# Gate logits with rows of x as the weights, a later place for four low parts, and one earlier quarter of W2: a fused attention and experts kernel

## The chip, the cores and the metric

One core of one Trainium2 chip runs the whole program. The metric is the device time of one execution in microseconds (us); the median of three runs is given. Five engines work from queues of their own: TensorE (PE, with its weight loads shown apart as PEld), VectorE (DVE), ScalarE (ACT), GpSimd (POOL) and SyncE (SP), which issues the DMAs here.

## The reference, cut to what matters

```python
# attention: batch 4, heads 8, sequence 576, head size 64, 128 features
def phi(x):
    proj = np.einsum('bhsd,df->bhsf', x, w_phi)
    proj = proj - np.max(np.abs(proj), axis=-1, keepdims=True)
    return np.concatenate([np.exp(proj), np.exp(-proj)], axis=-1)
q_p, k_p = phi(q), phi(k)
kv, z = np.einsum('bhsf,bhsd->bhfd', k_p, v), np.sum(k_p, axis=2)
num = np.einsum('bhsf,bhfd->bhsd', q_p, kv)
den = np.einsum('bhsf,bhf->bhs', q_p, z)[..., None] + 1e-06
x = num / den                      # as 2304 tokens x 512
# gated MLP
x = ((x @ w1) * (x @ w2) @ w3) @ w_out      # w1, w2 512x1024, w3 1024x1024, w_out 1024x512
# experts: 8 of them, every token goes through all
P = np.exp(x @ w_gate - (x @ w_gate).max())  # w_gate 512x8; then 8 rounds of row and column scaling
out = sum(P[:, e:e+1] * (np.maximum(x @ w1[e], 0) @ w2[e]) for e in range(8))  # w1[e] 512x1024, w2[e] 1024x512
```

## The kernel before, in words

Every float32 matrix is split into a high part in the reduced format fp32r and a low part (the difference), and a product is three fp32r matmuls: high x high, low x high, high x low (`mm3`, lines 84 to 87). ACT mostly makes the high part (`copy`), DVE the low one (`subtract`).

**Attention** (to about 214.6 us) goes through steps of three sequence tiles, k and q in turn. PE projects (`pp`), DVE takes the largest absolute value and the difference (`m`, `d`, in `st_M`), ACT makes the exponentials (`e`), PE sums `kv`. For q, PE transposes `d` (`dt`), ACT makes `q`, PE makes the denominators `dn` and the numerators `nu`. ACT copies each finished `kv` out of PSUM as `kh` and `kz`. PSUM banks of one pool of four turn among `kv`, `dt`, `dn` and `nu`. Beside it, the program already prepares the weights of the MLP: `get_w12(n)` for n below NW = 4 unpacks a weight into a ring of buffers (`wring`), makes its high part `wH` on ACT and its low part `wL` on DVE.

**Gated MLP** (214.6 to 531 us): six blocks j of 384 tokens. In each, 8 units `ab_unit(j, ft)` multiply x (its high and low parts XH and XL) with w1 and w2, then `px` matmuls give the new x, which ACT and DVE split again into XH and XL. `logits` follows: for each of four pieces of x's 512 rows the 16 columns of the split gate (`WG`) are the weights and 384 tokens of x move through (`lg`); DVE copies the 16x384 result (`lgs`), and PE transposes it in three pieces into one PSUM tile `lp`, tokens by gates. Blocks 0, 1 and 2 do so after their px matmuls, blocks 3 to 5 together after the last block.

**Experts**: units u, each one quarter of an expert's hidden layer, in chunks of 768 tokens. Units 0 to 15 are experts 0 to 3 of chunk 0 (531 to 785 us). From unit 16 (`NUC`) on, W2 is also taken in quarters: a quarter K11, K21 or K22 is loaded raw (`load_k`), split into a tile `t` (`load_t`) and stored for the later chunks. One raw buffer (`kr`) serves all of them. `products(u)` does seven products of Strassen's kind (a11, s2, s3, s1, a22, a12, s4); its weights `w_u_0` and `w_u_1` come by DMA, `w_u_2` is converted in the kernel (`get_w1(u, 2)`), behind an earlier copy by `issue_after(first[0])`. `part` then makes the split hidden operands `ah`, `al`, `bh`, `bl`, `dh`, `dl`, `eh`, `el` of the unit. After every fourth unit (p = 3) PE multiplies those of all four with the tiles t, group by group: first K11 with ah and al, then K21 with bh and bl. The raw `w_19_2` lies in a quarter of the tile MT, as it did before.

The order within each engine's queue is that of the program text, moved by priorities of a scheduler; `tc.issue_after(x)` keeps an instruction behind x.

Of the kernel before, what the change touches and what calls it, by code (L numbers as in the profile page):

```python
# [8 lines left out]
F32 = mybir.dt.float32  # L9
# [13 lines left out]
def f32(ap):  # L23
    return ap.bitcast(F32)
# [3 lines left out]
def kernel(  # L28
# [49 lines left out]
    def x_at(p, kt, c0, n):  # L78
        i, o = divmod(c0, NH)
        return XHL[i][p][:, kt, o : o + n]  # L80
# [15 lines left out]
    def subtract(key, out, a, b, i=0):  # L96
        engine(key, i).tensor_tensor(out, a, b, ALU.subtract)
# [565 lines left out]
    with ExitStack() as c2:  # L663
# [19 lines left out]
        def w12_piece(n):  # L683
            ft, w = divmod(n, 2)
            if n < NW:
                t = W12E[n]
            else:
                r = rb.tile([P, DF], U32, name=f"rw{n}", tag="r")
                nc.sync.dma_start(r, w12i[ft][:, w * DM : (w + 1) * DM].bitcast(U32))
                r = r.rearrange("p (n x) -> p n x", x=2)  # L690
                t = ring()
                u = t.bitcast(U32)
                with tc.issue_after(last["k"]):
                    nc.scalar.activation(t, r[:, :, 1].bitcast(F32), AF.Copy, scale=2.0**-112)
                nc.vector.tensor_scalar(
                    u, u, 3, 0x7FFFFFFF, ALU.logical_shift_left, ALU.bitwise_and
                )
                nc.vector.scalar_tensor_tensor(
                    u, r[:, :, 0], 29, u, ALU.logical_shift_right, ALU.bitwise_or
                )  # L700
                nc.vector.scalar_tensor_tensor(
                    u, r[:, :, 1], 0x80000000, u, ALU.bitwise_and, ALU.bitwise_or
                )
            pool = w12a if n < 9 else w12p
            hi = pool.tile([P, KT, P], F32R, name=f"wH{n}")
            lo = pool.tile([P, KT, P], F32R, name=f"wL{n}")
            t = t.rearrange("p (k f) -> p k f", k=KT)
            copy("wh", hi, t, n)
            subtract("wl", lo, t, f32(hi), n)
            w12[n] = hi, lo  # L710

        def get_w34(i):
# [15 lines left out]
            nc.vector.tensor_tensor(WG[:, :, 1], wg, f32(WG[:, :, 0]), ALU.subtract)  # L728

        def logits(blocks):  # L730
            got = []
            for j in blocks:
                ps = px_p.tile([P, N1], F32, name=f"lg{j}", tag="px")[0 : 2 * NE]
                for kt in range(KT):
                    w = WG[:, kt].rearrange("p a e -> p (a e)")
                    nc.tensor.matmul(ps, w, x_at(0, kt, j * N1, N1), start=kt == 0, stop=False)
                    nc.tensor.matmul(ps, w, x_at(1, kt, j * N1, N1), start=False, stop=kt == KT - 1)
                lg = xt_p[-1].tile([P, N1], F32, name=f"lgs{j}", tag="xt" if len(xt_p) == 1 else "lg")[0 : 2 * NE]
                nc.vector.tensor_copy(lg, ps)
                got.append((j, lg))  # L740
            for j, lg in got:
                for i in range(N1 // P):
                    nc.tensor.transpose(
                        lp[:, j * N1 // P + i].rearrange("p a e -> p (a e)"),
                        lg[:, i * P : (i + 1) * P],
                        ident[0 : 2 * NE, 0 : 2 * NE],
                    )

        cH = [cp.tile([P, N1], F32R, name=f"cH{i}") for i in range(FT)]
        cL = [cp.tile([P, N1], F32R, name=f"cL{i}") for i in range(FT)]  # L750
# [29 lines left out]
        for j in range(NT // N1):  # L780
            c0 = j * N1
            CH = [*zip(cH, cL)]
            if j == 1:
                CH[0] = cE
            for ft in range(FT):
                if j == 1 and ft == 0:
                    continue
                behind = ab_unit(j, ft, *CH[ft])
                if j == 0 and ft == FT // 2:
                    ab_unit(1, 0, *cE)  # L790
                if j > 0 and (ft < FT - 1 if 1 < j < NT // N1 - 1 else j == 1 or ft % 2 == 0):
                    sum_next(behind)
            if c0 + N1 == NT:
                assert made[0] == len(jobs)
                c7.close()
                c3.close()
                xt_p.append(sbuf(c2, "xt6", KT))
                xc = sbuf(c4, "xc", side="left")
                wc1 = sbuf(c4, "wc1", 2, "left")
                rwb = sbuf(c4, "rwb", side="left")  # L800
                c6 = c4.enter_context(ExitStack())
                rw1 = sbuf(c6, "rw1", 2, "left")
                load_w1(0)
                load_w1(1)
                prep_x(0, sbuf(c2, "xs0").tile([P, 2, N1], F32, name="xs0"))
                for u in range(2):
                    for i in range(3):
                        get_w1(u, i)
            if j == 0:
                get_gate()  # L810
            for dt in range(KT):
                ps = px_p.tile([P, N1], F32, name=f"px{j}_{dt}", tag="px")
                dc = slice(dt * P, (dt + 1) * P)
                for ft in range(FT):
                    hi, lo = w34[ft]
                    mm3(ps, hi[:, dc], lo[:, dc], *CH[ft], ft == 0, ft == FT - 1)
                xt = xt_p[-1].tile([P, N1], F32, name=f"xt{j}_{dt}", tag="xt")
                nc.scalar.copy(xt, ps)
                i, o = divmod(c0, 2 * N1)
                nc.sync.dma_start(XS[i][:, dt, o : o + N1], xt)  # L820
                xh, xl = x_at(0, dt, c0, N1), x_at(1, dt, c0, N1)
                nc.scalar.copy(xh, xt)
                with tc.high_priority(60) if c0 + N1 == NT else nullcontext():
                    behind = nc.vector.tensor_tensor(xl, xt, f32(xh), ALU.subtract).ins
                if 0 < j < NT // N1 - 1:
                    sum_next(behind)
            if c0 < NH:
                logits([j])
            elif c0 + N1 == NT:
                logits(range(NH // N1, NT // N1))  # L830
            if j == 0:
                c5.close()
                tq.append(sbuf(c7, "tq", 2))
                for k in range(3):
                    sum_load(k)
            if c0 + N1 == NH:
                cx[0].close()
                ones = sbuf(c4, "on", side="left").tile([P, P], F32, name="ones")
                nc.vector.memset(ones, 1.0)
                rx = sbuf(c4, "rx", side="left")  # L840
                load_x(0)
                tq.append(sbuf(c7, "tq1", 2, "left"))
                turn[0] = made[0]
                for k in range(3):
                    sum_load(made[0] + 3 + k)
# [5 lines left out]
    with c4:  # L851
# [49 lines left out]
        def products(u, bank, between):  # L901
# [17 lines left out]

            product("a11", B11, (c11, None))  # L920
            if NUC < u + 1 < NU and (u + 1) % NP > 1:
                with tc.issue_after(first[0]):
                    get_w1(u + 1, 2)
            product("s2", T2, (c12, c11))
            product("s3", T3, (c21, c12))
# [126 lines left out]

        rawK = {}

        def load_k(e, k):
            if e == NE:
                return
            r = rawK[e, k] = kr.tile([P, NP, DH], F32, name=f"k{e}_{k}", tag="k")
            j, h = KB[k]
            w = moe2_w2[e].rearrange("(j n p) (h d) -> j h p n d", j=2, p=P, h=2)[j, h]  # L1060
            nc.sync.dma_start(r, w)
# [7 lines left out]
        def load_t(u, k, taken=False):  # L1069
            s, e, p = units[u]  # L1070
            if not taken:
                take_t(u, k)
            t = TK[k]
            if s > 0 or k not in KB:
                nc.sync.dma_start(f32(t), W2S[e][:, WK[k]])
                return
            r = rawK.pop((e, k))
            copy("W2h", t[:, :, 0], r)
            subtract("W2l", t[:, :, 1], r, f32(t[:, :, 0]))
            load_k(e + (k == K22), {K11: K21, K21: K22, K22: K11}[k])  # L1080
            nc.sync.dma_start(W2S[e][:, WK[k]], f32(t))

        LATE = []
# [41 lines left out]
        def operands(u):  # L1125
            for i, c in enumerate(products(u, lambda n: bank(n)[:, 0:N1], lambda behind: None)):
                part(u, i, c)
# [9 lines left out]
        for u, (s, e, p) in enumerate(units):  # L1137
            if u < NUC:
                continue
            if p == 0:  # L1140
                take_mt(u)
                load_w1(u + NP - 1)
            operands(u)
            store_ready()
            if p < NP - 1:
                if u == NUC:
                    for k in (K11, K21, KT4):
                        take_t(u, k)
                    load_t(u, KT4, True)
                elif u < NUC + NP:  # L1150
                    load_t(u, (None, K11, K21)[p], True)
                elif p < 2:
                    load_t(u, p + 1)
                continue
# [155 lines left out]
```

## Time and profile before

| what | value |
|---|---|
| median of 3 runs | 1982.31 us (1982.3 to 1982.49) |
| profiled execution | 1983.45 us |
| its span, first to last instruction | 1981.7 us |
| PE busy | 1962.0 us (99%), 14037 matmuls |
| PE weight loads busy | 1874.9 us (95%) |
| DVE busy | 1471.1 us (74%) |
| ACT busy | 828.4 us (42%) |
| granted TensorE clock | 1.000 |

The span is what the trace covers; the profiled execution is 1.75 us longer. Busy is the union of an engine's instructions; the weight loads run beside the matmuls and are counted apart. The shares are means over stages that differ.

### The profile page before, as it was taken

Reading aid. Unit: us, or ns where it says so; the run is one execution under the profiler, and the core shown is the slowest. Engines: PE = TensorE matmul, PEld = TensorE weight load, DVE = VectorE, ACT = ScalarE, POOL = GpSimd, SP = SyncE. Lnnn points to the kernel's source line nnn. Section 1 sums busy time; section 2 is a strip of 40 time slices with the busy share of each in tenths; the row PEclk is TensorE's granted clock in tenths of the full one; section 3 lists DMA queues with packets and bytes.
Section 4 is the critical chain, followed back from the end, with each engine's and each line's share of the span. In section 5 each row is a group of like instructions: output and inputs, shape, how many; then the busy total and the mean of one; then the engine's idle time right before and its main releaser. Section 6 shows DMA issues by size and latency. Waiting matters only on the chain.

```text
span 1981.7 us, 35200 instructions
## 1 busy us (share of the span) xinstructions
PE 1962.0 (99%) x14037; PEld 1874.9 (95%) x14037; DVE 1471.1 (74%) x2546; ACT 828.4 (42%) x1539; POOL 93.2 (5%) x122
## 2 busy tenths in 40 slices
PE   8999999999999999999999999999999999999999
PEld 6677899999988988999999999999999999999999
DVE  7977946676798666888786777666788666777666
ACT  6866723344434432444343433333444333433333
POOL 2543100000000000000000000000000000000000
PEclk9999999999999999999999999999999999999999
DMA  6452538899899889888887777777778777777774
GB/s 224 161 168 94 170 138 288 309 312 330 305 349 333 291 320 315 306 290 307 314 307 269 245 250 246 251 245 254 246 276 283 244 245 253 245 250 252 244 247 150
DMA packets 187011, 511.55 MB, mean 258 GB/s; under 512 B 13792, under 2 KB 68960, under 8 KB 168800
## 3 DMA queue, kind: packets, MB, share of 16 engines
q1 hardware_dynamic: 186480, 508.88, 74.6%
q8 instruction: 111, 1.82, 0.4%
q10 hardware_dynamic: 368, 0.43, 0.1%
q14 instruction: 52, 0.43, 0.1%
HBM read 371.88 MB, written 137.36 MB: 257 GB/s over the span
## 4 chain that ended last, share of the span: by engine, by line
PE 89%; DVE 5%; DMA 3%; ACT 1%; issue 1%; SPq 0%; POOL 0%; DVEq 0%; ACTq 0%
PE ps L85 6%; PE ps L87 6%; PE ps L86 6%; PE pa L85 5%; PE pa L86 5%; PE pa L87 5%; PE b L1181 4%; PE b L1183 4%; PE b L1182 4%; PE ab L87 3%; PE ab L85 3%; PE ab L86 3%; PE a L1181 3%; PE a L1183 3%; PE a L1182 3%; PE py L86 2%
## 5 line engine op out<-in xcount | busy, mean ns | idle before, releaser
L917 DVE TENSOR_TENSOR c<-c,ps 128x384 f32<-128x384 f32 x480 | 255.8, 549 | 56.4 <-PE ps L87 53.8
L1202 DVE SCALAR_TENSOR_TENSOR o<-mt,Pw,o 128x512 f32<-128x512 f32 x108 | 75.1, 747 | 142.2 <-ACT mt L1192 142.2
L915 ACT COPY c<-pa 128x384 f32<-128x384 f32 x96 | 45.6, 475 | 228.2 <-PE pa L87 175.8
L1181 PE MATMUL b<-t,dh 128*128 128x256 f32 x480 | 136.0, 283 | 0.0
L1182 PE MATMUL b<-t,dh 128*128 128x256 f32 x480 | 135.8, 283 | 0.0
L1183 PE MATMUL b<-t,dl 128*128 128x256 f32 x480 | 135.8, 283 | 0.0
L87 PE MATMUL ab<-XH,wL 128*128 128x384 f32 x384 | 130.1, 339 | 0.0
L85 PE MATMUL ab<-XH,wH 128*128 128x384 f32 x384 | 130.0, 338 | 0.0
L86 PE MATMUL ab<-XL,wH 128*128 128x384 f32 x384 | 130.0, 338 | 0.0
L1108 ACT ACTIVATE c<-c 128x384 f32<-128x384 f32 x80 | 42.0, 525 | 169.8 <-DVE c L917 169.8
L917 DVE TENSOR_TENSOR c<-c,pa 128x384 f32<-128x384 f32 x192 | 103.6, 550 | 10.6 <-PE pa L87 9.6
L1181 PEld LDWEIGHTS b<-t,dh 128*128 128x128 f32 x480 | 92.1, 192 | 0.3 <-ACT mt L1192 0.3
L1183 PEld LDWEIGHTS b<-t,dl 128*128 128x128 f32 x480 | 92.2, 192 | 0.0
L1182 PEld LDWEIGHTS b<-t,dh 128*128 128x128 f32 x480 | 92.1, 192 | 0.0
L1181 PE MATMUL a<-t,eh 128*128 128x256 f32 x320 | 90.7, 283 | 0.7 <-DMA t<-w2s 0.7
L1183 PE MATMUL a<-t,el 128*128 128x256 f32 x320 | 90.6, 283 | 0.0
L1182 PE MATMUL a<-t,eh 128*128 128x256 f32 x320 | 90.5, 283 | 0.0
L1095 DVE SCALAR_TENSOR_TENSOR bl<-c,bh 128x768 fp32r<-128x768 f32 x80 | 76.3, 953 | 10.1 <-ACT bh L1094 10.1
L86 PE MATMUL py<-w,hH 128*128 128x512 f32 x192 | 76.3, 398 | 0.0
L87 PE MATMUL py<-w,hL 128*128 128x512 f32 x192 | 76.1, 397 | 0.0
L85 PE MATMUL py<-w,hH 128*128 128x512 f32 x192 | 75.5, 397 | 0.0
L1094 ACT ACTIVATE bh<-c 128x768 fp32r<-128x768 f32 x80 | 67.7, 846 | 14.3 <-DVE c L917 13.7
(287 smaller groups left out, 6513.5 us busy)
## 6 DMA issues: line engine op xcount, KB each, us to landing
t<-w2s SPq DMA_DIRECT2D x128, 1024.0 KB, 4.8
w<-w1s SPq DMA_DIRECT2D x160, 512.0 KB, 5.0
w<-w1s SPq DMA_DIRECT2D x64, 768.0 KB, 6.1
tr<-in_moe_w_dram SPq DMA_DIRECT2D x48, 512.0 KB, 5.2
w1s<-w SPq DMA_DIRECT2D x32, 768.0 KB, 7.4
w1s<-w SPq DMA_DIRECT2D x32, 512.0 KB, 7.9
w2s<-w SPq DMA_DIRECT2D x48, 256.0 KB, 7.8
w2s<-t SPq DMA_DIRECT2D x12, 1024.0 KB, 7.5
```

The source lines that it names most:

```text
L85: nc.tensor.matmul(ps, aH, bH, start=start, stop=False)
L86: nc.tensor.matmul(ps, aH, bL, start=False, stop=False)
L87: return nc.tensor.matmul(ps, aL, bH, start=False, stop=stop).ins
L915: first[0] = nc.scalar.copy(o, ps).ins
L917: nc.vector.tensor_tensor(o, t, ps, ALU.add)
L1094: nc.scalar.activation(hi, src, AF.Relu)
L1095: nc.vector.scalar_tensor_tensor(lo, src, 0.0, f32(hi), ALU.max, ALU.subtract)
L1108: nc.scalar.activation(c22, c22, AF.Relu)
L1181: nc.tensor.matmul(dst[i], H[:, c], T[:, 0], start=f, stop=False, skip_group_check=True)
L1182: nc.tensor.matmul(dst[i], H[:, c], T[:, 1], start=False, stop=False, skip_group_check=True)
L1183: nc.tensor.matmul(dst[i], L[:, c], T[:, 0], start=False, stop=l, skip_group_check=True)
L1202: nc.vector.scalar_tensor_tensor(o, src[i], w, o, ALU.mult, ALU.add)
```

## The change

Three edits. `logits` no longer takes the gate as the weights: each tile of 128 tokens of x (high, then low part, four pieces) is loaded as weights and the 16 gate columns move through, so that tokens by gates come out directly in `lp`; the transposes and the copies `lgs` are gone. Logits of blocks 0 and 1 are issued after the second unit of the next block. The low parts of the first four weights of `get_w12` are issued after the last `d` of attention. In chunk 0, for expert 4, the raw quarter K21 is loaded into free columns of MT ahead of the unit and K22 into the raw buffer; K11 and K21 are converted around unit 16 rather than in units 16 to 18, and `w_19_2` no longer waits for the copy.

```diff
--- before.py
+++ after.py
@@ -706,7 +706,8 @@
             lo = pool.tile([P, KT, P], F32R, name=f"wL{n}")
             t = t.rearrange("p (k f) -> p k f", k=KT)
             copy("wh", hi, t, n)
-            subtract("wl", lo, t, f32(hi), n)
+            with tc.issue_after(last["d"]) if n < NW else nullcontext():
+                subtract("wl", lo, t, f32(hi), n)
             w12[n] = hi, lo
 
         def get_w34(i):
@@ -728,23 +729,12 @@
             nc.vector.tensor_tensor(WG[:, :, 1], wg, f32(WG[:, :, 0]), ALU.subtract)
 
         def logits(blocks):
-            got = []
-            for j in blocks:
-                ps = px_p.tile([P, N1], F32, name=f"lg{j}", tag="px")[0 : 2 * NE]
+            for t in (j * N1 // P + i for j in blocks for i in range(N1 // P)):
+                o = lp[:, t].rearrange("p a e -> p (a e)")
                 for kt in range(KT):
                     w = WG[:, kt].rearrange("p a e -> p (a e)")
-                    nc.tensor.matmul(ps, w, x_at(0, kt, j * N1, N1), start=kt == 0, stop=False)
-                    nc.tensor.matmul(ps, w, x_at(1, kt, j * N1, N1), start=False, stop=kt == KT - 1)
-                lg = xt_p[-1].tile([P, N1], F32, name=f"lgs{j}", tag="xt" if len(xt_p) == 1 else "lg")[0 : 2 * NE]
-                nc.vector.tensor_copy(lg, ps)
-                got.append((j, lg))
-            for j, lg in got:
-                for i in range(N1 // P):
-                    nc.tensor.transpose(
-                        lp[:, j * N1 // P + i].rearrange("p a e -> p (a e)"),
-                        lg[:, i * P : (i + 1) * P],
-                        ident[0 : 2 * NE, 0 : 2 * NE],
-                    )
+                    nc.tensor.matmul(o, x_at(0, kt, t * P, P), w, start=kt == 0, stop=False)
+                    nc.tensor.matmul(o, x_at(1, kt, t * P, P), w, start=False, stop=kt == KT - 1)
 
         cH = [cp.tile([P, N1], F32R, name=f"cH{i}") for i in range(FT)]
         cL = [cp.tile([P, N1], F32R, name=f"cL{i}") for i in range(FT)]
@@ -788,6 +778,8 @@
                 behind = ab_unit(j, ft, *CH[ft])
                 if j == 0 and ft == FT // 2:
                     ab_unit(1, 0, *cE)
+                if c0 < NH and ft == min(j, 1) and j > 0:
+                    logits([j - 1])
                 if j > 0 and (ft < FT - 1 if 1 < j < NT // N1 - 1 else j == 1 or ft % 2 == 0):
                     sum_next(behind)
             if c0 + N1 == NT:
@@ -824,7 +816,7 @@
                     behind = nc.vector.tensor_tensor(xl, xt, f32(xh), ALU.subtract).ins
                 if 0 < j < NT // N1 - 1:
                     sum_next(behind)
-            if c0 < NH:
+            if c0 + N1 == NH:
                 logits([j])
             elif c0 + N1 == NT:
                 logits(range(NH // N1, NT // N1))
@@ -919,7 +911,7 @@
 
             product("a11", B11, (c11, None))
             if NUC < u + 1 < NU and (u + 1) % NP > 1:
-                with tc.issue_after(first[0]):
+                with tc.issue_after(first[0]) if u + 1 != NUC + NP - 1 else nullcontext():
                     get_w1(u + 1, 2)
             product("s2", T2, (c12, c11))
             product("s3", T3, (c21, c12))
@@ -1052,10 +1044,12 @@
 
         rawK = {}
 
-        def load_k(e, k):
+        def load_k(e, k, r=None):
             if e == NE:
                 return
-            r = rawK[e, k] = kr.tile([P, NP, DH], F32, name=f"k{e}_{k}", tag="k")
+            if r is None:
+                r = kr.tile([P, NP, DH], F32, name=f"k{e}_{k}", tag="k")
+            rawK[e, k] = r
             j, h = KB[k]
             w = moe2_w2[e].rearrange("(j n p) (h d) -> j h p n d", j=2, p=P, h=2)[j, h]
             nc.sync.dma_start(r, w)
@@ -1077,7 +1071,10 @@
             r = rawK.pop((e, k))
             copy("W2h", t[:, :, 0], r)
             subtract("W2l", t[:, :, 1], r, f32(t[:, :, 0]))
-            load_k(e + (k == K22), {K11: K21, K21: K22, K22: K11}[k])
+            if e > EARLY[0]:
+                load_k(e + (k == K22), {K11: K21, K21: K22, K22: K11}[k])
+            elif k != K21:
+                load_k(e + (k == K22), {K11: K22, K22: K11}[k])
             nc.sync.dma_start(W2S[e][:, WK[k]], f32(t))
 
         LATE = []
@@ -1139,16 +1136,22 @@
                 continue
             if p == 0:
                 take_mt(u)
+                if u == NUC:
+                    r = MT[0][:, 0:2].rearrange("p a n -> p (a n)")[:, 0 : NP * DH]
+                    load_k(e, K21, r.rearrange("p (a n) -> p a n", a=NP))
                 load_w1(u + NP - 1)
+                if u == NUC:
+                    for k in (K11, K21, KT4):
+                        take_t(u, k)
+                    load_t(u, KT4, True)
+                    load_t(u, K11, True)
             operands(u)
             store_ready()
             if p < NP - 1:
                 if u == NUC:
-                    for k in (K11, K21, KT4):
-                        take_t(u, k)
-                    load_t(u, KT4, True)
+                    load_t(u, K21, True)
                 elif u < NUC + NP:
-                    load_t(u, (None, K11, K21)[p], True)
+                    pass
                 elif p < 2:
                     load_t(u, p + 1)
                 continue
```

What stands on PE at the end of block 5, before the first product of unit 0 (pa, a11): the last logits matmuls and the transposes before, then the same place of the change.

```order
2160 L736 MATMUL lg_6047<-XH_68,WG 16x384
2161 L737 MATMUL lg_6047<-XL_69,WG 16x384
2162 L736 MATMUL lg_6047<-XH_68,WG 16x384
2163 L737 MATMUL lg_6047<-XL_69,WG 16x384
2164 L743 MATMUL lp<-ident,lgs_6034 128x16 x3
2165 L743 MATMUL lp<-ident,lgs_6045 128x16 x3
2166 L743 MATMUL lp<-ident,lgs_6056 128x16 x3
2167 L85 MATMUL pa_6130<-a11h_5843,w_0_2_5883 128x384
```

```order
2235 L736 MATMUL lp<-WG,XH_68 128x16
2236 L737 MATMUL lp<-WG,XL_69 128x16
2237 L736 MATMUL lp<-WG,XH_68 128x16
2238 L85 MATMUL pa_6190<-a11h_5873,w_0_2_5913 128x384
2239 L86 MATMUL pa_6190<-a11l_5874,w_0_2_5913 128x384
2240 L737 MATMUL lp<-WG,XL_69 128x16
2241 L736 MATMUL lp<-WG,XH_68 128x16
2242 L87 MATMUL pa_6190<-a11h_5873,w_0_2_5913 128x384
2243 L85 MATMUL pa_6190<-a11h_5873,w_0_2_5913 128x384
2244 L737 MATMUL lp<-WG,XL_69 128x16
```

The 24 matmuls of 384 columns and nine transposes became 72 of 16 columns. The later ones stand among the first matmuls of unit 0; this piece shows where they begin to.

What stands on ACT at the end of attention, behind the last cast of the four weights `wH` (e_2801 is the exponential of the last k piece, kh_2859 and kz_2860 are the copies of head pair 15's kv, L694 unpacks further weights into the ring), before and then in the change.

```order
221 L94 COPY kh_2804<-kv_2738 128x256
222 L94 COPY kz_2805<-kv_2738 128x128
223 L226 ACTIVATE q_2647<-dt_0_2775 128x2x192 x2
224 L226 ACTIVATE q_2781<-dt_1_2782 128x2x192 x2
225 L94 CAST XH_68<-x_2588 128x576
226 L205 ACTIVATE e_2801<-d_2731 128x768 x2
227 L694 ACTIVATE wring<-rw_3022 128x512
228 L694 ACTIVATE wring<-rw_3045 128x512
229 L694 ACTIVATE wring<-rw_3073 128x512
230 L94 COPY kh_2859<-kv_2808 128x256
231 L94 COPY kz_2860<-kv_2808 128x128
232 L226 ACTIVATE q_2781<-dt_0_2845 128x2x192 x2
```

```order
221 L205 ACTIVATE e_2801<-d_2731 128x768 x2
222 L226 ACTIVATE q_2647<-dt_0_2775 128x2x192 x2
223 L226 ACTIVATE q_2781<-dt_1_2782 128x2x192 x2
224 L94 CAST XH_68<-x_2588 128x576
225 L94 COPY kh_2804<-kv_2738 128x256
226 L94 COPY kz_2805<-kv_2738 128x128
227 L694 ACTIVATE wring<-rw_3022 128x512
228 L226 ACTIVATE q_2781<-dt_0_2845 128x2x192 x2
229 L694 ACTIVATE wring<-rw_3045 128x512
230 L226 ACTIVATE q_2781<-dt_1_2851 128x2x192 x2
231 L94 CAST XH_68<-x_2689 128x576
232 L94 COPY kh_2859<-kv_2808 128x256
```

The exponential moved to the front, and the copies kh and kz of both head pairs moved behind activations for q; those of pair 15 now stand behind the cast XH_68 of x_2689 too.

What stands on SP in chunk 0 when the loads of unit 18's weights (w_18_0, w_18_1) come (k_0, k_1 and k_5 are the raw quarters K11, K21 and K22 of expert 4, mt_8376 and mt_8436 the tile MT), before and then in the change.

```order
393 L1061 DMA k_0_8374<-in_moe_w_dram 128x4x256
394 L559 DMA mt_8376<-in_moe_w_dram 128x768
395 L1075 DMA t_4_2_8464<-w2s_167 128x2048
396 L574 DMA w_18_0_8412<-w1s_4_119 128x2x512
397 L574 DMA w_18_1_8422<-w1s_4_119 128x2x512
398 L1061 DMA k_1_8558<-in_moe_w_dram 128x4x256
399 L1081 DMA w2s_167<-t_4_0_8462 128x2048
```

```order
393 L1055 DMA k_0_8434<-in_moe_w_dram 128x4x256
394 L1055 DMA mt_8436<-in_moe_w_dram 128x4x256
395 L559 DMA mt_8436<-in_moe_w_dram 128x768
396 L1069 DMA t_4_2_8441<-w2s_167 128x2048
397 L1055 DMA k_5_8445<-in_moe_w_dram 128x4x256
398 L1078 DMA w2s_167<-t_4_0_8439 128x2048
399 L574 DMA w_18_0_8482<-w1s_4_119 128x2x512
400 L574 DMA w_18_1_8492<-w1s_4_119 128x2x512
```

K21 is now read into MT, ahead of the weights of unit 19, and K22 and the store of t_4_0 moved ahead of the loads of unit 18's weights.

## Rows read from the trace of the kernel before

**Rows 1.** Windows: busy us of each engine, granted clock, DMA share, GB/s.

```profile
216.00:530.00 314.00, 312.47 (x1783) 306.62 (x1781) 214.77 (x423) 125.55 (x222) 0.94 (x4) 1.00 0.77 265
...
796.00:824.00 28.00, 26.19 (x167) 25.23 (x166) 26.54 (x49) 14.71 (x23) 0.00 (x0) 1.00 0.81 297
```

**Rows 2.** Waits of PE, 140 to 1060 us: us in total, times, longest.

```profile
PE kv L249 <- ACT e L205: 1.2, 2, 0.8
```

**Rows 3.** Timeline of PE, blocks 1 and 3 to 5: start us, us, instruction.

```profile
317.69 0.34 PE L87 MATMUL px<-cH,woL 128*128 128x384 f32 x1
...
323.83 0.34 PE L86 MATMUL ab<-XL,wH 128*128 128x384 f32 x1
...
525.15 0.34 PE L87 MATMUL px<-cH,woL 128*128 128x384 f32 x1
...
531.37 0.34 PE L85 MATMUL pa<-a11h,w 128*128 128x384 f32 x1
```

**Rows 4.** Weight loads (PEld) by line and form: busy us, mean ns.

```profile
L85 PEld LDWEIGHTS ab<-XH,wH 128*128 128x128 f32 x384 | 72.1, 188 | 0.7 <-issue 0.4
...
L249 PEld LDWEIGHTS kv<-v,e 128*64 128x64 f32 x1152 | 38.6, 137 | 5.1 <-ACT e L205 2.0 <-DVE t L292 1.2 <-issue 0.2
```

**Rows 5.** Timeline of PEld around lp and mb; their loads' ns (min/median/max).

```profile
376.45 0.26 PEld L743 LDWEIGHTS lp<-ident,lgs 16*128 16x128 f32 x3 [0.25 <-DVE lgs L739]
376.74 0.19 PEld L86 LDWEIGHTS ab<-XL,wH 128*128 128x128 f32 x1
...
L743 PEld LDWEIGHTS lp<-ident,lgs x18: 133/136/138, 272.6 to 530.6; 16*128 16x128 f32 x18
...
534.19 0.29 PEld L964 LDWEIGHTS mb<-m,ones 1*128 1x128 f32 x2 [0.25 <-DVE m L960]
...
L964 PEld LDWEIGHTS mb<-m,ones x2: 181/182/184, 534.2 to 534.3; 1*128 1x128 f32 x2
```

**Rows 6.** Timelines of DVE, ACT and PE at the end of attention.

```profile
199.91 2.50 DVE L97 TENSOR_TENSOR wL<-wring,wH 128x512 fp32r<-128x512 f32 x4 [0.69 <-ACT wH L94]
...
207.77 0.27 ACT L94 COPY kz<-kv 128x128 f32<-128x128 f32 x1
...
209.33 2.16 PE L305 MATMUL nu<-q,kh 128*64 128x288 f32 x16
```

**Rows 7.** Timelines of PE and DVE in units 16 to 19 and the first groups.

```profile
806.83 0.34 PE L87 MATMUL ps<-s4h,w 128*128 128x384 f32 x1
...
808.73 0.33 PE L85 MATMUL pa<-a11h,w 128*128 128x384 f32 x1
...
816.80 0.38 PE L1181 MATMUL a<-t,ah 128*128 128x256 f32 x1 [1.15 <-ACT c L915]
...
825.54 0.28 PE L1181 MATMUL d<-t,bh 128*128 128x256 f32 x1
...
787.99 1.22 DVE L97 TENSOR_TENSOR t<-k,t 128x1024 fp32r<-128x1024 f32 x1
...
791.61 0.55 DVE L917 TENSOR_TENSOR c<-c,pa 128x384 f32<-128x384 f32 x1 [0.35 <-PE pa L87]
...
797.31 1.01 DVE L917 TENSOR_TENSOR c<-c,ps 128x384 f32<-128x384 f32 x2
...
800.39 0.55 DVE L1120 SCALAR_TENSOR_TENSOR c<-c 128x384 f32<-128x384 f32 x1
...
815.23 0.95 DVE L1101 TENSOR_TENSOR dl<-c,dh 128x768 fp32r<-128x768 f32 x1
```

**Rows 8.** Loads of w at L574, 789 to 791 us, then 797 to 798.

```profile
L574 SPq DMA_DIRECT2D w<-w1s x2: 524/524/524, 789.5 to 790.6; - x2
...
DMA to landing us min/median/max: 4.6/6.2/7.8
...
L574 SPq DMA_DIRECT2D w<-w1s x2: 524/564/605, 797.4 to 798.0; - x2
...
DMA to landing us min/median/max: 8.9/9.3/9.6
```


## The prediction

> **What bounds the kernel.** First the page's busy times, in the table above: TensorE (PE) is the engine that hardly rests, so what counts is each microsecond that its instruction stream gains or loses; work of the other engines counts where PE waits for it. Then the windows: in the gated MLP (216 to 530 us) PE is busy 312.47 of 314 us, and in 796 to 824, where the change touches the experts, 26.19 of 28, with VectorE (DVE) busy 26.54 of those 28; the granted clock is 1.00, the 2.4 GHz level, in both [rows 1]. The list of waits names one whose cause this change moves, kv for the exponentials e, 1.2 us [rows 2]; another shows in the timeline of the experts, 1.15 us of the first W2 group for a copy c [rows 7]. The profiled execution takes 1983.45 us, 1.75 more than its span; the median of the runs shown is 1982.31. Sums below are differences, added to that median. Runs differ by 0.2 us, but I call a change real from 0.2%, about 4 us: under 1978.3 is faster, over 1986.3 slower.
>
> **Part 1, the gate logits: what is removed.** I read PE's time from the last px matmul ahead of the logits to a matmul behind them and take off the others at their pitch (ab 0.1765, px and pa 0.1725 us). Blocks 3 to 5: 525.15 to 531.37 is 6.22; one px and three pa between cost 0.69 and leave 5.5, of which 24 logits matmuls fill 4.1 and the rest is transposes and two waits for lgs [rows 3]. Block 1: 317.69 to 323.83 is 6.14; one px and sixteen ab take 3.0, leaving 3.14, a wait for lgs in it [rows 3]. Blocks 0 and 2 have the same pattern and, read in the same way, give 2.0 and 2.5. Removed: 13.1 us.
>
> **What is added.** 18 token tiles x 4 x 2 = 144 pairs of a weight load (a 128x128 piece of x) and a matmul of 16 columns, 72 of them for blocks 3 to 5 straight ahead of unit 0 or among its first matmuls. Sixteen columns cannot cover a load of 128, so the pair costs what a load costs when nothing hides it. No row shows a plain 128x128 load so exposed; the nearest:
> - mb, 128 columns of one row, one moving column: two loads are busy 0.29 in all at 0.182 for one, so the second starts 0.108 behind the first [rows 5].
> - lp, 128 columns of 16 rows, 16 moving, near the new matmul's shape but transposing: three loads and the next product's, 376.45 to 376.74, are 0.097 each; by their busy time alone, 0.26 less one load of 0.136, over two, 0.062 [rows 5].
> - loads of 64 columns last 137 ns and of 128 columns 188 ns [rows 4]: 0.80 ns a column, 0.102 for 128.
> - an upper bound is the pitch of 256-column matmuls, whose load is hidden: 72 from 816.80 to 825.54, 0.121 [rows 7].
>
> I take 0.108: mb's load lasts about as long as those of 128x128 (182 against 188), lp's is a shorter kind (136). 144 x 0.108 = 15.6, net +2.4 us; the bounds 0.062 and 0.121 give -4.2 and +4.3. Breaking even needs 0.091.
>
> The Trainium skill, "TensorE: Matmul & The Clock Gate", section "LDWEIGHTS (loading the stationary operand)", has a load take its column count over 1.2 in ns, about 107 for 128 columns; that speaks against the change, the slope of rows 4 agrees with it, and by it the net would be +2.3. The same page, section "Back-to-back issue gap", gives 81 ns as the sustained spacing of pairs with 128 moving columns.
>
> Six copies of lgs leave DVE, where nothing on the path gains from it. Logits 0 and 1 move behind the second unit of the next block, long after their x is split. I expect no new wait.
>
> **Part 2, the end of attention.** The first four low parts of w12 hold DVE from 199.91 to 202.41, ahead of m and d of the last k piece but one; behind them e, then kv, which loses 1.2 [rows 2, 6]. With them behind the last d that 1.2 us goes: e can run about 1.5 us earlier and kv ends about 206.2. What is late next: the subtractions now run at about 205.2 to 207.7, and ScalarE's (ACT) next weights (L694, into the same ring) wait for them. In the changed order two L694, four q and one XH stand ahead of kh and kz of head pair 15, where before three L694 did. From 205.9: 0.6 + 0.9 + 0.6 + 0.9 + 0.6 + 0.6 for kh and kz ends at about 210.2; before, kz ended at 208.04 [rows 6]. PE's first nu writes the PSUM bank that kz reads, so it starts at about 210.25 rather than 209.33 [rows 6]; what follows it has no slack, so all of it shifts. Net +0.9. Bounds: -1.2 if kz is early enough, +1.3 if one more L694-sized operation is in the way. The low parts themselves are needed from 214.6 on, seven us later.
>
> **Part 3, chunk 0, expert 4.** Two losses could go: unit 19's first product waits for its late weights (806.83 to 808.73 holds four 0.1725 pitches, so 1.2 us), and group K11 for a copy behind DVE's dl, 1.15 up to 816.80 [rows 7]. K21's conversion, ahead of those weights on DVE, moves to unit 16, and w_19_2 goes up by some 6 us: the first goes, and PE would reach K11 at 814.4, 2.4 earlier. But K11 then needs unit 19's own ah and al in program order, where before PE ran on with K21's matmuls. From 800.39, just behind unit 17's last evacuation, the changed DVE order has 27 instructions of the 0.55 us kind, which follow each other every 0.47 (two in 1.01), and 7 of the 0.95 kind, taken at the same 0.08 less, up to that al: 18.8 us, so 819.2, with stalls 819.6 [rows 7]. K11 waits there with 43 of its and K21's 72 matmuls still to go (5.2 at 0.121), so these end at about 824.9 against 825.54: -0.6.
>
> A second trouble is on SyncE's queue. The load of K22 now stands ahead of unit 18's two loads, and takes the one k buffer: it waits for the subtraction of t_4_0 (1.22 us), which moves from 787.99 to behind unit 16's last pa evacuation (791.61), so to about 793.3 [rows 7]. So w_18_0 and w_18_1, issued from 789.5 on before, go out at about 794.3 and 794.9, behind 0.5 MB of load and 1 MB of store. The two before landed after 4.6 and 7.8 us; two issued behind such a store, at 797.4 and 798.0, after 9.6 and 8.9 [rows 8]. The first is harmless (799.5), 7.8 makes PE wait 1.9 us from 800.8, where unit 18's second product starts (35 pitches ahead of 806.83), and 8.9 makes it 3. Up to 1.9 are swallowed, since PE would wait for al anyway; beyond, each us costs one. Part 3: -0.4, bounds -2.4 (neither trouble) and +1.2.
>
> **Sum.** +2.4 + 0.9 - 0.4 = +2.9: 1985.2 us (1986.35 for the profiled execution).
>
> **The rivals.**
> - *Loads overlap* (faster). If the 144 pairs run at 0.062 as lp's busy time allows, the logits give -4.2. With the tail at its bound -1.2 and part 3 at -2.4 the total is 1974.5; with my tail and part 3, 1978.6. It decides at a pitch of some 0.06. For it: PE loads the next weights beside a running matmul all through the kernel. Against: lp's pitch from start to start is 0.097.
> - *Middle spacing*. The two loads and matmuls overlap by a part, 0.081 for a pair, between lp's two readings: 11.7, net -1.4, sum 1981.4, no change that can be told. The 0.081 is also the spacing that the Trainium skill names in "Back-to-back issue gap" of "TensorE: Matmul & The Clock Gate"; here lp's starts bear 0.097 instead.
> - *All three cost* (slower). Pairs at 0.121 (+4.3), kz as computed (+0.9), w_18_1 landing after 9.6 (+1.2): 1988.7. It is slower from a pitch of about 0.113 with part 3 at zero; what decides is the exposed load, the others only lift it.
> - *The change doesn't do what it says*: e is early but nu waits for kz, K11 is early but waits for al. Those two alone, with equal logits, leave 1982.8.
>
> **How the numbers follow.** My forecast (pitch 0.09 to 0.117, the troubles of parts 2 and 3 in it) holds 0.45 and ends at 1982.7 to 1986.6, 0.03 of it above 1986.3; middle spacing 0.10, by the starts of lp; overlap 0.20, 0.17 of it faster; all cost 0.25. The range takes in overlap with my other parts and the slower rival, and leaves out some 2 in 10: 1978.3 to 1988.8. Faster 0.17, same 0.55, slower 0.28.
>
> **What the new profile would show.** The lp matmuls at about 0.108 from start to start, and no lgs; none in a wait. kv with no wait for e, but the first nu about 0.9 later and waiting for ACT's kz. PE without the wait for w_19_2; a wait of 1 to 2 us in K11 for ah or al, or one for w<-w1s in unit 18 near 801. It would be wrong if the pairs stream at a load's hidden rate, or if the interleaved ones (17 in block 2, about as many in unit 0) each cost a drain besides, some 0.1 us and so +3.

## The result: slower by 0.7%, outside the range

The changed kernel takes 1997.49 us (median of 6 runs, 1995.33 to 2000.9) against 1982.90 for the kernel before in the same series (6 runs, 1982.3 to 1984.01): a ratio of 1.0074 [1.0061, 1.0087]. The profiled execution takes 1995.33 us at a span of 1993.5; before it was 1983.45 and 1981.7.

The windows of the changed kernel (busy us of PE, PEld, DVE, ACT and POOL with their instructions, then granted clock, DMA share, GB/s) cover the two stretches of [rows 1], and inside them the run of logits ahead of unit 0 and the second product of unit 18.

```profile
216.00:530.00 314.00, 313.93 (x1818) 313.33 (x1817) 212.85 (x419) 126.23 (x219) 0.19 (x1) 0.99 0.77 264
527.00:531.40 4.40, 4.40 (x42) 4.40 (x40) 2.96 (x6) 0.99 (x2) 0.00 (x0) 1.00 0.94 276
531.40:545.20 13.80, 13.80 (x56) 13.15 (x56) 2.33 (x7) 0.48 (x1) 0.00 (x0) 0.51 1.04 401
545.20:560.00 14.80, 14.80 (x87) 14.79 (x88) 13.36 (x35) 9.14 (x14) 0.00 (x0) 1.00 0.65 220
796.00:824.00 28.00, 24.88 (x134) 24.45 (x133) 22.57 (x39) 13.39 (x22) 0.00 (x0) 0.94 0.79 304
814.50:818.30 3.80, 3.73 (x12) 3.73 (x13) 3.77 (x7) 0.94 (x2) 0.00 (x0) 0.55 1.00 413
```

The granted clock is the third column from the end. Where before it read 1.00 in both stretches, it now reads 0.51 for 13.8 us, the 1.2 GHz level, while PE is busy in all of those 13.80 us. The stretch holds the end of the 72 pairs for blocks 3 to 5 and the first matmuls of unit 0. A mean of 0.99 over 314 us hides a second fall (0.57 in 330 to 334, behind block 1's 24 pairs).

PE's timeline shows what the pairs cost at each level, and the wait in unit 18:

```profile
527.09 0.26 PE L737 MATMUL lp<-WG,XL 128*128 128x16 f32 x1
527.20 0.26 PE L736 MATMUL lp<-WG,XH 128*128 128x16 f32 x1
...
531.45 0.26 PE L736 MATMUL lp<-WG,XH 128*128 128x16 f32 x1
531.56 0.36 PE L737 MATMUL lp<-WG,XL 128*128 128x16 f32 x1
531.77 0.36 PE L736 MATMUL lp<-WG,XH 128*128 128x16 f32 x1
...
814.57 0.46 PE L85 MATMUL ps<-s2h,w 128*128 128x384 f32 x1 [3.12 <-DMA w<-w1s]
814.86 0.50 PE L86 MATMUL ps<-s2l,w 128*128 128x384 f32 x1
```

Up to 531.56 the pairs follow each other every 0.111 us, close to mb's 0.108 in [rows 5]; from there every 0.21. The matmuls of 384 columns, which go at 0.1725 before, take 0.29 and more behind the wait at 814.57.

The other places of the prediction: in attention's tail the two waits of kv for e [rows 2] are gone, and nu waits instead, for ACT's q:

```profile
207.77 2.52 PE L305 MATMUL nu<-q,kh 128*64 128x288 f32 x16 [0.83 <-ACT q L226]
...
212.82 1.19 PE L305 MATMUL nu<-q,kh 128*64 128x288 f32 x8 [0.30 <-DVE t L292]
```

On SyncE's queue, K22's load and the store of t_4_0 go out just ahead of unit 18's two loads, which land 7.0 and 9.0 us after their issue, the later of them like the late ones of [rows 8] (8.9 and 9.6):

```profile
803.84 0.38 SPq L1055 DMA_DIRECT2D k<-in_moe_w_dram  x1
804.26 0.51 SPq L1078 DMA_DIRECT2D w2s<-t  x1
804.87 2.54 SPq L574 DMA_DIRECT2D w<-w1s  x2
```

To see where the time is lost I set the starts of the same PE instructions in two traces against each other. This ledger (start in the kernel named, less the start before, us) is worked out from the timelines:

```
                         after    e1      f1      f2      f3      g4
first ab                 -0.67   -0.81   -0.79   -1.17   -0.44   -0.35
last px of block 0       -0.30   -0.81   -0.25   -1.17   -0.43   -0.35
last px of block 2       +1.43   +2.45   -0.10   -0.98   +2.82   +2.88
last px of block 5       +1.74   +2.85   +5.65   +4.19   +8.60   +3.29
unit 0, second product   +8.34  +10.46   +1.07   +7.17   +4.03   +3.12
unit 4, second product  +10.55  +11.80   +3.16  +16.06   +6.09   +3.12
unit 18, second product +13.80  +11.76   +3.09  +16.11   +6.02   +3.12
unit 19, second product +14.31  +10.56   +6.35  +14.22   +9.44   +3.48
last matmul             +11.86  +12.00   +6.18  +13.78   +9.06   +5.71
```

Of the 11.86 us, 11.22 are lost between attention and unit 4, where only the logits changed; 0.37 of them arise in block 0, ahead of the first logits matmul.

### The profile page after: what moved, and what is told of

Same layout as the page of the kernel before. It is cut to its first block, busy times and chain, and to the rows that moved or that the text cites. A ratio compares the mean times of both kernels' runs of the same rounds, so it can differ in the third digit from the quotient of the medians.

```text
span 1993.5 us, 35349 instructions
## 1 busy us (share of the span) xinstructions
PE 1974.8 (99%) x14115; PEld 1893.5 (95%) x14115; DVE 1469.7 (74%) x2540; ACT 827.7 (42%) x1539; POOL 93.2 (5%) x122
## 4 chain that ended last, share of the span: by engine, by line
PE 94%; DVE 3%; DMA 1%; ACT 1%; issue 1%; POOL 0%; DVEq 0%
PE ps L85 7%; PE ps L86 7%; PE ps L87 7%; PE pa L85 5%; PE pa L86 5%; PE pa L87 5%; PE b L1184 4%; PE b L1186 4%; PE b L1185 4%; PE ab L85 3%; PE ab L87 3%; PE ab L86 3%; PE a L1184 3%; PE a L1186 3%; PE a L1185 3%; PE py L86 2%
```

## The experiments

**The theories.** A: the logits make the loss, and in them the granted clock more than the exposed loads. Its rival: the loads alone, with the tail and chunk 0 (C) making the rest. Each expectation says itself what its letters stand for.

**First, one part at a time.** The kernel before with hunks 1 to 3 of the diff alone (the logits; the end of them is shown):

```diff
...
-            if c0 < NH:
+            if c0 + N1 == NH:
                 logits([j])
```

> Only the logits of the change, all else as before. Theory A (the clock): the 144 pairs cost 0.111 us each, 16.0 in all for the 13.1 removed, so +2.9, and the runs of 16-column matmuls are followed by stretches at a granted clock of 0.50, one of some 3 us behind block 1's pairs and one of some 14 us around unit 0, which add 1.6 and 6.2: +10.7 in all, and between +8 and +15 if the stretches differ from run to run. Theory B (the exposed load alone): +2.9, and the clock stays at 1.00 once the experts' late weights are gone from the program.

Measured: 1995.73 us (5 runs), 1.0066 [1.0053, 1.0079]. The logits alone make nearly all of the loss. The windows of this kernel (columns as above) show three stretches at the lower clock:

```profile
275.20:279.10 3.90, 3.90 (x16) 3.90 (x16) 0.47 (x2) 0.00 (x0) 0.00 (x0) 0.56 0.63 206
330.40:333.70 3.30, 3.30 (x12) 3.30 (x12) 0.66 (x2) 0.00 (x0) 0.00 (x0) 0.52 0.78 212
531.20:545.90 14.70, 14.70 (x65) 14.32 (x64) 1.66 (x5) 0.48 (x1) 0.00 (x0) 0.54 1.04 403
```

Length times (1 - clock) is what each stretch lost: 3.9 x 0.44, 3.3 x 0.48 and 14.7 x 0.46 give 1.7, 1.6 and 6.8, about 10 us by this rough count. The ledger's loss from attention to unit 4 is 12.6 (-0.81 to +11.80).

The low parts' new place alone (hunk 0):

```diff
-            subtract("wl", lo, t, f32(hi), n)
+            with tc.issue_after(last["d"]) if n < NW else nullcontext():
+                subtract("wl", lo, t, f32(hi), n)
```

> Only the four low parts behind the last difference. By the trace of the changed kernel the first ab starts at 213.95 rather than 214.62, of which 0.37 is lost again in block 0: -0.3 to -0.7 us. By the prediction on record (nu waits for the copy kz): +0.9.

Measured: 1983.76 us (11 runs), 1.0007 [0.9998, 1.0016]: no change that can be told. PE reaches the first ab 0.88 earlier, and has lost 1.1 again by the end of block 0. But e1, whose attention is that of before, also reaches ab 0.81 earlier: profiles differ there by as much, so the gain of the tail isn't shown.

Chunk 0 alone (the diff's last hunks, a piece of which is shown), and chunk 0 with the tail (the whole change with the old logits):

```diff
...
+            if e > EARLY[0]:
+                load_k(e + (k == K22), {K11: K21, K21: K22, K22: K11}[k])
+            elif k != K21:
+                load_k(e + (k == K22), {K11: K22, K22: K11}[k])
...
```

> Only the part of the change in chunk 0. Theory C (queue): unit 18's second product waits about 3.3 us for its weights, whose loads stand behind the raw K22 and a store, and the clock falls to 0.50 for some 3.7 us behind that wait (1.85 more), for 2.4 gained: +2 to +3 us. By the prediction on record, in which up to 1.9 us of the wait are swallowed by the wait of K11: between -0.4 and +1.2.

> The changed kernel with the logits of before. If the parts add, +1.5 to +2.5 us (e2 and e3 together), and the logits are then what is left of the whole change, 10 to 13 us. If the two other parts lose by themselves more than that, theory A has to give up as much.

Measured: 1982.57 us (11 runs), 1.0002 [0.9993, 1.0011], and 1983.35 (11 runs), 1.0002 [0.9993, 1.0011]. The 2 to 3 us that the late weights of unit 18 were to cost are missing in both. SyncE's timeline in chunk 0 alone shows why:

```profile
789.68 0.38 SPq L1063 DMA_DIRECT2D k<-in_moe_w_dram  x1
790.10 0.51 SPq L1086 DMA_DIRECT2D w2s<-t  x1
790.70 2.48 SPq L574 DMA_DIRECT2D w<-w1s  x2
```

K22's load goes out at 789.68, not 803.84. Of this difference 11.0 us are only that the whole change runs later by then (unit 16's second product at 796.67, here at 785.62). The other 3.1 come from the scheduler, which here put the subtraction of t_4_0, for which the load waits, at 788.43 on DVE; in the whole change it stands at 802.60, behind the last evacuation of unit 16. With the old logits and the rest of the change it stands early too, at 790.11 with unit 16's second product at 787.30: it is the new logits that move it. The rest of chunk 0 goes as computed: K11 waits for al,

```profile
819.17 0.39 PE L1194 MATMUL a<-t,al 128*128 128x256 f32 x1 [0.48 <-DVE al L1100]
```

and the group behind it starts at 824.18 rather than 825.54, with 0.53 gained before: -0.8, where -0.6 was computed.

**Where the clock falls.** f1 to f3 stand on e1, f4 on e3. f1 spreads the pairs, 8 of one token tile at a time behind units 1, 3 and 5 of the next block:

```diff
-        def logits(blocks):
+        def logits(blocks, part=range(N1 // P)):
...
+                if j not in (0, NH // N1) and ft in (1, 3, 5):
+                    logits([j - 1], [ft // 2])
```

> The logits of the change alone, the same 144 pairs, but those of blocks 0, 1, 3 and 4 are issued a token tile at a time (8 pairs, 0.9 us) behind three units of the next block; blocks 2 and 5 keep their 24 at their end, partly among other matmuls. Theory A (a long run of 16-column matmuls lowers the clock): no stretch at 0.50, and only the exposed loads are left, +2.9 us. Theory B' (the clock answers to the pairs themselves, wherever they stand): +10 or more, as with the logits in the order of the change.

Measured: 1989.98 us (5 runs), 1.0035 [1.0023, 1.0048]. In the windows of the profiled execution the lower clock is gone from all the logits:

```profile
216.00:530.00 314.00, 313.72 (x1833) 313.12 (x1832) 207.99 (x410) 124.32 (x218) 0.27 (x1) 1.00 0.75 261
526.00:565.00 39.00, 38.87 (x233) 38.07 (x232) 35.18 (x83) 20.88 (x34) 0.00 (x0) 1.00 0.98 361
```

The same 144 pairs now cost 3.4 us from the end of block 0, ahead of all logits, to unit 4 (-0.25 to +3.16), where e1's cost 12.6 (-0.81 to +11.80). So some 9.2 us of e1's loss are the clock, and 3.4 the loads. Blocks 4 and 5 add 2.67 each for 24 pairs among full-size matmuls, 0.111 a pair: no drain on top. The other 3 us come later, where the first product of unit 19 waits 2.98 for a cast of w that this schedule places late, and the clock falls behind it (0.72 in 813 to 817):

```profile
813.25 0.45 PE L85 MATMUL pa<-a11h,w 128*128 128x384 f32 x1 [2.98 <-ACT w L94]
```

The profiled execution has a mean clock of 0.999, which that one fall makes up. Two of the other four have 0.998 and 0.997, so there the clock fell more often, and where isn't known.

f2 keeps e1's order, but lets each pair move 128 columns (WG's 16 repeated eight times; a copy on DVE takes one of the eight):

```diff
-                    w = WG[:, kt].rearrange("p a e -> p (a e)")
+                    w = WG[:, kt].rearrange("p a e -> p (a e)").unsqueeze(1).to_broadcast([P, P // 16, 2 * NE])
...
+                nc.vector.tensor_copy(lp[:, t].rearrange("p a e -> p (a e)"), o[:, 0])
```

> The logits of the change alone in its places, but the 16 gate columns move through eight times in each matmul, 128 columns, into a bank of their own, and DVE copies 16 of the 128 to lp: same number of loads, same pitch (128 columns last about 0.05 us, hidden under the 0.111 of a load), eight times the columns. Theory A' (the clock answers to how much of the array's time moves columns): no stretch at 0.50, +2.9 us. Theory D (it answers to the exposed loads): as with 16 columns, +10 or more, with 72 pairs in one run here.

Measured: 1997.18 us (5 runs), 1.0065 [1.0052, 1.0078]. The time as a whole is not what was expected, since two falls came behind waits of PE: 1.28 us for XH at 372.75, in the middle of block 2's pairs, and 4.51 for DVE's c up to 550.64. What the run was for stands in PE's timeline and the windows: the first of these holds all of the 72 pairs (529.52 to 537.97), the others the long wait and the fall.

```profile
535.74 0.28 PE L735 MATMUL lg<-WG,XH 128*128 128x128 f32 x1
535.85 0.27 PE L736 MATMUL lg<-WG,XL 128*128 128x128 f32 x1
535.96 0.28 PE L735 MATMUL lg<-WG,XH 128*128 128x128 f32 x1
```

```profile
529.50:538.00 8.50, 8.25 (x75) 8.11 (x73) 4.29 (x14) 1.00 (x2) 0.00 (x0) 1.00 1.01 340
545.00:551.00 6.00, 1.49 (x9) 1.17 (x8) 2.10 (x5) 1.57 (x2) 0.00 (x0) 1.00 0.86 327
551.00:557.60 6.60, 5.20 (x18) 4.69 (x17) 5.32 (x17) 4.57 (x7) 0.00 (x0) 0.50 0.61 215
```

The pairs have the same pitch of 0.11, and the clock is 1.00 throughout, though the 72 are less broken up than e1's, of which the last 19 stand among matmuls of unit 0; one wait of 0.25 us is all that parts them. The runs of 24 behind blocks 0 and 1 bring no fall either (1.00 in 270 to 285 and in 330 to 345). What differs from e1 in those runs is how many columns move, besides the bank that they write and DVE's copies. That f2's waits brought the clock down is read from its trace; it wasn't tried apart. For the short one it is doubtful, since the waits of 1.07 and 1.15 in the kernel before have no fall behind them; what brought that fall is open.

f3 leaves each block's 24 pairs in one piece, but takes blocks 3 to 5 apart:

```diff
...
+                if j not in (0, NH // N1) and ft == 1:
+                    logits([j - 1])
...
-                logits(range(NH // N1, NT // N1))
+                logits([j])
```

> The logits of the change alone, each block's 24 pairs behind the second unit of the next block (blocks 2 and 5 at their end as in the change). Theory A, with the length of the run deciding: the 72-pair run's stretch of 14 us is gone; after 24 pairs the clock fell behind block 1 and not behind block 0 in the profiled execution, so each run may cost 1.6 or nothing: +2.9 to +11, likely some +6. Rival (the raw weights and transfers of unit 0, not the run, lower the clock there): the stretch stays around unit 0, +9 or more.

Measured: 1992.75 us (5 runs), 1.0048 [1.0035, 1.0060], between e1 and f1. In its windows two runs of 24 unbroken pairs bring the clock down (0.58 in 277 to 280.8, 0.52 in 331.3 to 334.5), and the end doesn't:

```profile
331.30:334.50 3.20, 3.20 (x12) 3.19 (x12) 0.18 (x1) 0.14 (x1) 0.00 (x0) 0.52 0.64 146
526.00:565.00 39.00, 38.88 (x234) 38.20 (x233) 35.19 (x80) 21.04 (x34) 0.00 (x0) 1.00 0.93 349
```

In the blocks without a fall the scheduler had broken the 24 into 6, 1 and 17, or smaller pieces. The rival, that unit 0's transfers lower the clock, is out: in 526 to 565 they move 349 GB/s at a clock of 1.00. A third fall (0.57 in 816 to 820) stands behind a wait of 2.88 us of unit 19's first product, like f1's.

f4 leaves the new logits out, and moves the old ones of blocks 0 and 1 behind the next block's second unit, with chunk 0's change (its issue points are shown):

```diff
...
+                if j in (1, 2) and ft == 1:
+                    logits([j - 1])
+                if j in (1, 2) and ft == 3:
+                    turned()
...
```

> The part of the change in chunk 0, with the logits of before, those of blocks 0 and 1 issued behind the second unit of the next block and their transposes behind the fourth, so that block 1's wait for lgs (1.07 in the trace of before) and the drains around it have time. Both theories: the clock stays at 1.00; -0.8 from chunk 0 and -1 from the wait, -2 us, about what can just be told.

Measured: 1981.58 us (11 runs), 0.9996 [0.9987, 1.0005]. In its ledger 2.0 us are gained by the end of block 2 and at the last matmul, but the runs don't tell it from the kernel before. Its median is the lowest of the versions.

**How much of the loss hangs on the long run, and on chunk 0.** g3 adds to e1 one matmul of 384 columns behind every fourth pair, into a tile that nothing reads:

```diff
+                    if kt % 2:
+                        ps = px_p.tile([P, N1], F32, name=f"fill{t}_{kt}", tag="px")
+                        nc.tensor.matmul(ps, x_at(0, kt, t * P, P), x_at(0, kt, t * P // N1 * N1, N1), start=True, stop=True)
```

> The logits of the change alone in its places, with work added: behind every 4 of the 144 pairs one matmul of 384 columns into a scratch bank that nobody reads, 36 in all. By count they add 36 x 0.17 = 6.2 us. Theory A' (the clock answers to the columns that move): the stretch of 14 us at 0.50 around unit 0 and those of blocks 0 and 1 go, so by the start of unit 4 the kernel stands at +2.9 + 6.2 = about +9 rather than +11.8, faster than without the added work. If the clock answers to the length of a run of exposed loads or to these loads at all, the stretches stay and it stands at +17.

Measured: 1998.90 us (4 runs), 1.0080 [1.0067, 1.0093], and +18.3 at unit 4, the dearer of the two forecasts. Behind blocks 0 and 1 the clock stays up, but in the run of 72 it falls all the same, for 20 us, as the windows show:

```profile
270.00:340.00 70.00, 70.00 (x418) 70.00 (x417) 38.29 (x86) 18.61 (x34) 0.00 (x0) 1.00 0.71 246
531.00:551.00 20.00, 20.00 (x85) 19.80 (x84) 1.27 (x5) 0.48 (x1) 0.00 (x0) 0.51 0.93 358
```

g4 has the new logits for blocks 0 to 2 and the old ones for 3 to 5 (the definition of `old_logits`, that of before, is left out):

```diff
...
-                logits(range(NH // N1, NT // N1))
+                old_logits(range(NH // N1, NT // N1))
```

> The new logits in blocks 0 to 2, those of before in blocks 3 to 5. Theory A, by the ledger of the logits alone: blocks 0 and 1 cost 0.6 for the loads and 1.6 to 1.8 for each stretch at 0.50 (one or two), block 2 some 0.4; the 72 pairs and their 14 us at 0.50 are gone: +2 to +5 in all, against +13 with them.

Measured: 1987.31 us (6 runs), 1.0028 [1.0016, 1.0039]. At unit 4 it stands at +3.12 where e1 stands at +11.80: blocks 3 to 5, with their 72 pairs, make 8.7 us.

g1 is the whole change with K22's load and t_4_0's store moved behind unit 16 (the hunk that takes them out of `load_t` is left out); g2 is g1 with f1's runs of 8:

```diff
...
+                    load_k(e, K22)
+                    nc.sync.dma_start(W2S[e][:, WK[K11]], f32(TK[K11]))
                     load_t(u, K21, True)
```

> The whole change, but the raw K22 is loaded and t_4_0 stored after unit 16 instead of ahead of it, so that SyncE issues the loads of unit 18's weights first, as before. Theory C (queue): the 3.1 us wait for them in unit 18 and the 3.7 us at a granted clock of 0.50 behind it go, -4 to -5 us against the change in that stretch (the trace from unit 18 to the first d), and the logits' 10 us stay: +8 to +11 in all. If the loads are late whatever stands ahead of them, the wait stays.

> The whole change with the logits in runs of 8 pairs and K22 later: both troubles that the traces showed are gone. Theories A and C: the clock stays at 1.00 throughout, the exposed loads cost 2.9 to 4, chunk 0 gives about 1 back: +2 to +3. If it is still +7 or more, the loss sits elsewhere.

Measured: 1997.58 us (6 runs), 1.0074 [1.0063, 1.0086], and 1992.06 (5 runs), 1.0048 [1.0035, 1.0061]. Neither gained what it was to gain. In both the wait of unit 18 is gone, as theory C has it, but unit 19 waits for its weights instead: 2.61 us in g1 at 825.74, where the clock stays up, and 4.55 in g2, again with a lower clock behind it (0.60 in 816 to 820):

```profile
816.47 0.41 PE L85 MATMUL ps<-s2h,w 128*128 128x384 f32 x1 [4.55 <-DMA w<-w1s]
```

The load and the store had gone from ahead of unit 18's weights to ahead of unit 19's. From unit 17 to the first d g1 loses 1.3 us in its trace where the changed kernel loses 2.4, 1.1 less instead of the 4 to 5 expected. At unit 4 g2 stands at +3.8, close to f1's +3.2, and no fall stands near its logits either.

The rest of g1's miss lies in the logits. Its profiled execution is the longest of its six (2002.02 us) and stands at +15.0 by unit 4: the fall behind block 1 lasts longer than in the changed kernel, and one more stands behind block 2, whose pairs are broken into 6, 1 and 17. The windows of these two, and of the wait in unit 19:

```profile
330.00:337.00 7.00, 7.00 (x25) 7.00 (x25) 1.54 (x4) 0.48 (x1) 0.00 (x0) 0.52 0.88 270
381.00:385.00 4.00, 4.00 (x16) 4.00 (x15) 2.13 (x5) 1.30 (x2) 0.00 (x0) 0.57 0.98 369
825.00:832.00 7.00, 6.26 (x36) 6.29 (x37) 7.00 (x13) 3.71 (x7) 0.00 (x0) 1.00 0.55 204
```

## Why the prediction was wrong, point by point

**The step that failed** is the one under all of part 1: it prices the new matmuls by their pitch alone, and takes the granted clock of 1.00 in [rows 1], a row of the old instructions, for the new ones too. The price of a pair was right: 0.108 said, 0.111 measured. From 0.111, 144 pairs take 16.0 us; f1's +3.4 then puts the removed work at 12.6 rather than 13.1. So the loads cost 3.4 us, 1.0 more than the forecast's +2.4. What the sum lacked is the clock. In the changed kernel, counted from the starts, 31 pairs take 0.204 rather than 0.111 (2.9 us), 19 matmuls of 384 columns 6.88 rather than 3.28 (3.6), and twelve ab behind block 1 3.65 rather than 2.12 (1.5): 8.0, which with the loads' 3.4 makes 11.4, against 10.9 in the ledger from the end of block 0 to unit 4. None of the rivals had it: the dearest was the exposed load at 0.121 with +4.3.

That the clock, and not the load, makes the difference is shown by f1 (the same pairs, 1.00 at all the logits, 9.2 us less). That the falls go with the 16 columns, and not with the pitch of the loads, is shown by f2's 72 pairs, at the same pitch and 1.00. What the length of a run does shows only as a tendency. In the profiled executions the clock fell in all three long runs of blocks 3 to 5 (changed kernel, e1, g1), behind 8 of 10 unbroken runs of 24, behind one of 12 that were broken into 6, 1 and 17 or smaller (g1's block 2), and behind no run of 8 (f1, g2). How much of other work keeps it up is not settled: g3's fillers did behind 24 pairs and didn't in 72. Nor is it settled why block 0's run brings the clock down in e1, f3 and g4, but not in the changed kernel and g1.

The Trainium skill, "TensorE: Matmul & The Clock Gate", section "What's actually happening", has the clock follow how busy PE has been recently, 1.2 GHz after idleness. Here the profile counts PE as busy in all 13.80 us at 0.51, so what the page calls busy is not what the profile counts. Its section "HAM oscillation — how this bites in real kernels" has waits for transfers bring the clock down; the 3.12 us wait at 814.57, with 0.55 behind it, agrees; g1's wait of 2.61 us has 1.00 behind it.

**The middle spacing and the overlap** (0.081 and 0.062) fell at once, since the pitch is 0.111, with 128 moving columns (f2) as with 16.

**Part 2** (+0.9): the wait of kv went, and nu did wait in its place, as said, but for q (0.83 and less), not for kz, and ab starts no later. What failed is the link from kz to nu: kz of head pair 15 did end late, at 210.05 where 210.2 was computed, but the first nu had started at 207.77, and only the dn at 210.22 stands behind that kz. In the time it is nothing: 1.0007 [0.9998, 1.0016].

**Part 3** (-0.4): the queue trouble was named rightly. Unit 18's loads landed 7.0 to 9.0 us after their issue and PE waited 3.12, the upper of the two cases (3 for 8.9). The loads were issued at 804.87, which less the 10.5 us that the kernel is late by then is the 794.3 that was computed. What was not foreseen is that the clock falls behind the wait (12 matmuls in 3.76 us, not 2.07), and that the whole trouble hangs on where the scheduler puts one subtraction: behind unit 16's last evacuation in the whole change, ahead of it in e3 and e4, though their chunk 0 is the same. In the ledger it costs 3.3 at unit 18, of which some 1.9 are given back by unit 68. From unit 16 to the end +1.3 is left, where -0.4 was forecast. It is thus a small part of the whole.

**The sum** was +2.9; the profiled execution shows +11.9 and the medians +14.6. The two differ because the changed kernel's own runs spread over 5.6 us, and the profiled one is the shortest.

## What to carry to other kernels

Before replacing wide matmuls by many narrow ones, ask what the granted clock does in a long run of them: here a pair cost just what its load costs, and then the clock fell and the full-size matmuls behind paid as well. Read the clock by windows of the stretch, since a mean of 0.99 hid falls to 0.50. If narrow matmuls are wanted, spread them in short runs among wide ones, as f1 did (here they still didn't pay: f1 takes 7.8 us more than the kernel before), and check in the timeline that a scheduler hasn't moved a wait elsewhere in return.

## What the runs showed of the hardware that was not expected

- PE fully busy by the profile, and the granted clock at 0.51 for 13.8 us, in a run of pairs with 16 moving columns and the first matmuls behind it; in a run of 72 pairs with 128 columns (f2), at the same pitch of 0.111, it stayed at 1.00.
- A pair of a 128x128 load and a matmul starts every 0.111 us whether it moves 16 or 128 columns; at the lower clock every 0.21.
- Behind waits of PE of 3.12 us (changed kernel) and 4.51 (f2) the clock was 0.55 and 0.50 for the next 4 to 7 us, so such a wait cost more than its length: 1.7 us more in the first case. Behind one of 2.61 us (g1) it stayed at 1.00.
